# Attention followed by an MoE-style layer: q and k in one transfer over 128 partitions plus a small rest, and a scheduler that assumes later landings

## The chip, the core and the metric

The kernel runs on one core of a Trainium2 chip. The metric is the device time of one execution in microseconds (us). All inputs and the output lie in the chip's memory (DRAM); the working memory has 128 partitions, and a transfer (DMA) writes rows of bytes into partitions.

## The reference

Everything is float32 except the two weights, which arrive as float64 and are turned into float32 on the chip.

```python
# q, k, v: (8 batches, 8 heads, 576, 64); p: (8, 8, 32, 64); scale = 1/8
p_packed = softmax(scale * p @ k.T) @ v          # 32 packed rows a head
out      = softmax(scale * q @ p_packed.T) @ p_packed
x = out.transpose(0, 2, 1, 3).reshape(8 * 576, 512)
h = x @ w_in                                     # 512 -> 2048
g = h * tanh(softplus(h))                        # mish
return g @ w_out                                 # 2048 -> 512
```

## The kernel before

Heads stand in two groups (g = 0, 1) of four. For one batch b and one group the kernel holds q and k transposed, in tiles named `xT` of 128 partitions by 4 x 320 columns. Partitions 0 to 63 hold the 64 features of the first 256 positions of the four heads, partitions 64 to 127 hold the same features of the remaining 320 positions. This is `PARTS = (0, 256), (256, 576)`; a loop over `u` walks the two parts. `load_turned` fetches such a tile with two transfers, one for each part: `k_a` (64 partitions, 4096 bytes in each, 256 KB) and `k_b` (64 partitions, 5120 bytes in each, 320 KB); `q_a` and `q_b` likewise. `load_v` fetches v as `v_main` (128 partitions of 4096 bytes, 512 KB) and `v_rest` (64 partitions of 1024 bytes, 64 KB). `load_p` fetches the packed queries (`pT`, 128 KB).

Attention of a batch: `products` (line 290) multiplies p with k into `ps_s`, or the packed values with q into `ps_s`/`ps_m`; row maxima, exponentials and sums follow on DVE and ACT; `turn_chunks` (L376, L377) turns the weights with matmuls against the identity; ACT copies them out (`a1T`, L386/L400); `values` (L413) multiplies by v; the result `pp` is turned into `ppT`. In batch 0 (method `first`, then `turned`) the products with q are copied out by ACT (L499), turned by PE (`ps_t`, L507), normalised row by row on DVE (L520 to L550) and turned by PE once more, from which ACT (L564) and DVE (L567) make `aT_hi` and `aT_lo`, a high and a low part of the attention weights. In the other batches (method `later`) DVE does the turning (L451, L574).

The layer after it is folded: `pack` (L668) multiplies `ppT` with four blocks of w_in (`wi`) into `ps_w`, from which ACT and DVE make `wp_hi` and `wp_lo`. A block of the layer is `up` (L748: `ps_h` from aT and wp, two halves of six matmuls), `gate` (L758: mish on ACT), `high` and `low` (g_hi, g_lo) and, two blocks later, `down` (L800 to L802: four chunks of three matmuls into `acc`). There are 16 blocks a batch; the 128 blocks run as batch 0 blocks 0 to 7, batch 1 blocks 0 to 15, batch 0 blocks 8 to 15, and then batches 2 to 7.

The weights come as float64 in tiles `w_st` of 128 partitions by 4096 bytes (512 KB). Each is converted by two instructions on ACT (L607, L611) and four on DVE (L614, L620, L624, L630); a w_out tile needs one more of each. There are 16 fetches of w_in and 16 of w_out. Converted w_in blocks are stored to DRAM (L633) and fetched again later (L660).

Every transfer is issued by one queue, SP. A transfer that reuses one of the eight completion counters first waits for the previous transfer on that counter, so about eight are in flight. The order of all instructions on PE, DVE, ACT and SP is made before the launch by a list scheduler, `Lineup`: `forward` walks through the operations with assumed costs and picks the next one for each engine. For a transfer it assumes that the data are there 500 ns after the time at which `wire` (a running sum of bytes over a rate) has passed; line 154 holds that number. The engines then run their queues strictly in that order; each instruction waits by semaphore for what it reads.

Of the kernel before, what the change touches and what calls it, by code (L numbers as in the profile page):

```python
# [8 lines left out]
F32 = mybir.dt.float32  # L9
# [27 lines left out]
class Lineup:  # L37
# [5 lines left out]
    AHEAD = 4000  # L43
    SWITCH = 1283
    STOP = 100
    ENGINES = ("PE", "DVE", "ACT", "SP")

    def __init__(self, slots):
# [51 lines left out]
    def forward(self, due):  # L100
        ops = self.ops
        free = {pool: [0.0] * n for pool, n in self.slots.items()}
        at = {e: 0.0 for e in self.ENGINES}
        wire, warm, table = 0.0, 0.0, "exp"
        begins, ends, tooks = {}, {}, {}
        left, left_users = [len(op["needs"] | op["behind"]) for op in ops], {k: set(v) for k, v in self.users.items()}
        pool_of, last = {}, {}
        est = {n: 0.0 for n, op in enumerate(ops) if not left[n]}
        while est:
            best = {}  # L110
            for n, begin in est.items():
                op = ops[n]
                begin = max(begin, at[op["engine"]])
                wanted = {}
                for pool, _ in op["takes"]:
                    wanted[pool] = wanted.get(pool, 0) + 1
                if any(len(free[pool]) < k for pool, k in wanted.items()):
                    continue
                for pool, k in wanted.items():
                    begin = max(begin, sorted(free[pool])[k - 1] + self.HOP)  # L120
                if op["engine"] == "SP":
                    begin = max(begin, wire - self.AHEAD, op["never_before"])
                cost = begin
                if op["table"] and op["table"] != table and due[n] > begin:
                    cost += self.SWITCH
                best.setdefault(op["engine"], []).append((cost, due[n], n, begin))
            if not best:
                raise RuntimeError("stuck: " + ", ".join(str(ops[n]["takes"]) for n in sorted(est)))
            picks = []
            for engine, found in best.items():  # L130
                first = min(found)[0]
                d, n, cost, begin = min((d, n, c, b) for c, d, n, b in found if c <= first + self.NEAR)
                picks.append((cost, d, n, begin))
            cost, _, n, begin = min(picks)
            op = ops[n]
            del est[n]
            took = op["cost"]
            tooks[n] = took
            if op["table"] and op["table"] != table:
                table = op["table"]  # L140
                begin += self.SWITCH
                tooks[n] += self.SWITCH
            if op["engine"] == "PE":
                if begin > at["PE"]:
                    took += self.STOP
                if begin - at["PE"] > 2500:
                    warm = begin + 4000
                if begin < warm:
                    took = min(2 * took, (took + (warm - begin) / 2) if begin + 2 * took > warm else 2 * took)
            begins[n] = begin  # L150
            at[op["engine"]] = begin + took
            if op["engine"] == "SP":
                wire = max(wire, begin + 1500) + op["lag"]
                ends[n] = wire + 500
            else:
                ends[n] = begin + took + op["lag"]
            for pool, k in op["takes"]:
                free[pool].remove(min(free[pool]))
                pool_of[k] = pool
            for k in op["uses"]:  # L160
                left_users[k].discard(n)
                last[k] = max(last.get(k, 0.0), ends[n])
                if not left_users[k]:
                    free[pool_of[k]].append(last[k])
            for m in op["after"]:
                left[m] -= 1
                if not left[m]:
                    est[m] = max((ends[w] + self.HOP for w in ops[m]["needs"]), default=0.0)
        assert len(begins) == len(ops), len(begins)
        return begins, ends, tooks  # L170
# [9 lines left out]
def body(  # L180
    ctx: ExitStack,
    tc: tile.TileContext,
    q_a: bass.AP,
    q_b: bass.AP,
    k_a: bass.AP,
    k_b: bass.AP,
    v_main: bass.AP,
    v_rest: bass.AP,
    pT: bass.AP,
# [5 lines left out]

    nc = tc.nc

    B, G, D, H4, CUT = q_a.shape  # L200
    NP = 32
    S = CUT + q_b.shape[4]
    HALF = S // 2
    PARTS = (0, CUT), (CUT, S)
    DF = w_in.shape[1]
    DO = w_out.shape[1]
    P = 128
    NF = DF // P
    FC = 512
    NCH = S // P  # L210
    MAIN = NCH * P
    REST = S - MAIN
    scale = 1.0 / float(D) ** 0.5
# [8 lines left out]
    ps_h = ctx.enter_context(tc.tile_pool(name="ps_h", bufs=1, space=bass.MemoryType.PSUM))  # L222
# [5 lines left out]
    make_identity(nc, ident)  # L228


    ps_warm = ps_h.tile([P, P], F32, name="ps_warm", tag="ps_x")

    wo = {i: const.tile([P, 2, DO], F32R, name=f"wo{i}") for i in range(NF // 2)}

# [15 lines left out]
    class Batch:  # L250
# [10 lines left out]

        def load_turned(self, ts, src, g):
            ts[g] = att.tile([P, H4 * (S - CUT)], F32, name="xT", tag="T", bufs=XB)
            for u, (a, e) in enumerate(PARTS):
                nc.sync.dma_start(
                    out=ts[g][u * D:(u + 1) * D, :H4 * (e - a)].rearrange("a (h t) -> a h t", h=H4), in_=src[u][self.b, g]
                )

        def load_k(self, g):
            self.load_turned(self.kT, (k_a, k_b), g)  # L270

        def load_q(self, g):
            self.load_turned(self.qT, (q_a, q_b), g)

        def load_v(self, g):
            t = self.v[g] = att.tile([P, NCH + 1, H4, D], F32, name="v", bufs=VB)
# [3 lines left out]
        def begin(self):  # L280
            self.a1 = att.tile([P, 2, S], F32, name="a1", tag="a", bufs=2)
            self.pp = att.tile([P, 2, 2, D], F32, name="pp")
            self.rs = stat.tile([P, 2], F32, name="rs")
            self.sums = stat.tile([P, 2, 2], F32, name="sums")
# [880 lines left out]
def by_slot(x):  # L1165

    import numpy as np

    x = np.asarray(x)
    b, h, s, d = x.shape  # L1170
    x = x.reshape(b, 2, h // 4, 2, s, d)
    return np.stack([x[:, 0], x[:, 1][:, :, ::-1]], axis=1).reshape(b, 2, 4, s, d)


def laid_out(q, k, v, p, moe_w_in, moe_w_out):

    import numpy as np

    def turned(x, a, e):
        return by_slot(x)[..., a:e, :].transpose(0, 1, 4, 2, 3)  # L1180

    s = q.shape[2]
    cut = s // 128 * 64
    vs = by_slot(v)
    b, g, h, _, d = vs.shape
    main = s // 128 * 128
    ps = by_slot(p).transpose(0, 4, 1, 2, 3).reshape(b, d, g, -1)
    return {
        "q_a": turned(q, 0, cut),
        "q_b": turned(q, cut, s),  # L1190
        "k_a": turned(k, 0, cut),
        "k_b": turned(k, cut, s),
        "v_main": vs[:, :, :, :main].reshape(b, g, h, main // 128, 128, d).transpose(0, 1, 4, 3, 2, 5),
        "v_rest": vs[:, :, :, main:].transpose(0, 1, 3, 2, 4),
        "pT": np.concatenate([ps, ps], axis=1),
        "w_in": moe_w_in,
        "w_out": moe_w_out,
    }
# [22 lines left out]
```

## Time and profile before

| | |
|---|---|
| median of 3 runs | 734.15 us (732.8 to 736.47) |
| the profiled execution | 735.77 us, span of the program in it 734.0 us |
| busy: PE, DVE, ACT | 712.8, 393.1, 301.3 us |
| granted TensorE clock, mean | 0.976 |
| bytes moved | 85.74 MB, mean 117 GB/s |
| q and k transfers | 64 in all (16 each of q_a, q_b, k_a, k_b) |

PE is TensorE, DVE VectorE, ACT ScalarE; "PEld" is the loading of weights into TensorE. The span is the time from the program's first to its last instruction; the profiled execution's own time is 1.8 us longer. A profile lists work by line of the kernel and by the names of the tiles (out<-in). "Idle before <-X" means that the engine stood still and that X ended the wait. A busy PE counts overlapping matmuls, so its busy time says that it had work, not that it ran at its peak.

### The profile page before, as it was taken

To read this page: it belongs to the slowest core of one execution; us is meant where nothing else is said; L and a number is where in the kernel's file an instruction comes from. 1 tells how busy PE (TensorE), PEld (TensorE's weight loads), DVE (VectorE), ACT (ScalarE), POOL (GpSimd) and SP (SyncE) were. 2 spreads that over 40 slices of the span, in tenths; PEclk is the share of its full clock that TensorE was granted. 3 is DMA by queue.
4 is the path that set the end of the run, shared out by engine and by line. 5 is a ranking of instruction groups with operands and counts; after the bars stand their busy time and mean duration, and the time that the engine had idled before them with its cause. 6 is when DMAs were issued, how large, how long until landed. Compare 5 with 4: busy or idle time off the path is not lost.

```text
span 734.0 us, 12404 instructions
## 1 busy us (share of the span) xinstructions
PE 712.8 (97%) x5058; PEld 572.0 (78%) x5058; DVE 393.1 (54%) x702; ACT 301.3 (41%) x718; POOL 0.7 (0%) x6
## 2 busy tenths in 40 slices
PE   6679999999999999999999999999999999999997
PEld 4267787878787878887788787877788787888886
DVE  4589988955743446353743537343564445542332
ACT  4488776543521434243422425225333254332221
POOL 0000000000000000000000000000000000000000
PEclk7579999999999999999999999999999999999999
DMA  9994066732318310671115611292013911130002
GB/s 266 276 320 171 6 225 203 223 98 80 115 44 226 119 50 9 190 183 59 58 58 150 183 57 58 60 274 97 7 52 116 270 61 58 58 115 1 1 1 72
DMA packets 27833, 85.74 MB, mean 117 GB/s; under 512 B 3712, under 2 KB 5760, under 8 KB 27776
## 3 DMA queue, kind: packets, MB, share of 16 engines
q1 hardware_dynamic: 27776, 84.95, 38.4%
q8 instruction: 40, 0.66, 0.4%
q14 instruction: 17, 0.14, 0.1%
HBM read 71.30 MB, written 13.63 MB: 116 GB/s over the span
## 4 chain that ended last, share of the span: by engine, by line
PE 88%; DMA 8%; ACT 2%; DVE 1%; issue 0%; SPq 0%; ACTq 0%
PE ps_h L748 27%; PE acc L800 16%; PE acc L801 15%; PE acc L802 15%; PE ps_w L668 4%; DMA w_st<-in_w_in_dram 4%; PE ps_rest L800 2%; PE ps_rest L801 2%; PE ps_rest L802 2%; PE ps_pp L413 2%; DMA xT<-in_k_b_dram 2%; DMA xT<-in_q_b_dram 1%; DMA w_st<-in_w_out_dram 1%; PE ps_m L290 1%; PE ps_s L290 1%; PE ps_a L376 1%
## 5 line engine op out<-in xcount | busy, mean ns | idle before, releaser
L758 ACT ACTIVATE g<-ps_h 128x288 f32<-128x288 f32 (+1 forms) x256 | 98.5, 386 | 295.5 <-PE ps_h L748 212.2
L800 PE MATMUL acc<-wo,g_hi 128*128 128x512 f32 x512 | 203.9, 398 | 0.0
L801 PE MATMUL acc<-wo,g_hi 128*128 128x512 f32 x512 | 201.7, 394 | 0.0
L802 PE MATMUL acc<-wo,g_lo 128*128 128x512 f32 x512 | 201.1, 393 | 0.0
L748 PE MATMUL ps_h<-aT_hi,wp_hi 128*128 128x288 f32 x512 | 155.7, 304 | 0.3 <-DVE a L451 0.3
L748 PE MATMUL ps_h<-aT_hi,wp_lo 128*128 128x288 f32 x512 | 151.7, 296 | 0.2 <-DVE wp_lo L685 0.2
L748 PE MATMUL ps_h<-aT_lo,wp_hi 128*128 128x288 f32 x512 | 151.4, 296 | 0.0
L766 DVE CAST g_hi<-g 128x512 fp32r<-128x512 f32 x112 | 47.3, 422 | 180.5 <-ACT g L758 180.2
L748 PEld LDWEIGHTS ps_h<-aT_hi,wp_hi 128*128 128x128 f32 x512 | 96.6, 189 | 34.9 <-issue 24.2
L802 PEld LDWEIGHTS acc<-wo,g_lo 128*128 128x128 f32 x512 | 96.0, 188 | 23.0 <-DVE g_lo L770 0.2
L800 PEld LDWEIGHTS acc<-wo,g_hi 128*128 128x128 f32 x512 | 96.0, 188 | 19.6 <-DVE g_hi L766 3.4
L801 PEld LDWEIGHTS acc<-wo,g_hi 128*128 128x128 f32 x512 | 96.1, 188 | 11.0
L748 PEld LDWEIGHTS ps_h<-aT_lo,wp_hi 128*128 128x128 f32 x512 | 96.7, 189 | 9.0
L748 PEld LDWEIGHTS ps_h<-aT_hi,wp_lo 128*128 128x128 f32 x512 | 96.7, 189 | 0.6 <-DVE wp_lo L685 0.6
L770 DVE TENSOR_TENSOR g_lo<-g,g_hi 128x512 fp32r<-128x512 f32 x128 | 88.3, 690 | 6.4 <-ACT g_hi L766 0.4
L685 DVE TENSOR_TENSOR wp_lo<-ps_w,wp_hi 128x512 fp32r<-128x512 f32 x64 | 41.6, 684 | 40.7 <-ACT wp_hi L680 40.6
L680 ACT CAST wp_hi<-ps_w 128x512 fp32r<-128x512 f32 x64 | 34.5, 590 | 40.6 <-PE ps_w L668 40.6
L668 PE MATMUL ps_w<-wi,ppT 64*32 64x512 f32 x512 | 36.7, 615 | 0.0
L760 ACT ACTIVATE g_rest<-ps_h 128x64 f32<-128x64 f32 x128 | 28.0, 219 | 0.0
L800 PE MATMUL ps_rest<-wo,r_hi 128*128 128x512 f32 x64 | 25.1, 392 | 0.0
L801 PE MATMUL ps_rest<-wo,r_hi 128*128 128x512 f32 x64 | 25.1, 392 | 0.0
L802 PE MATMUL ps_rest<-wo,r_lo 128*128 128x512 f32 x64 | 25.1, 392 | 0.0
(97 smaller groups left out, 566.9 us busy)
## 6 DMA issues: line engine op xcount, KB each, us to landing
wi<-w_in_f SPq DMA_DIRECT2D x48, 512.0 KB, 4.8
w_st<-in_w_in_dram SPq DMA_DIRECT2D x16, 512.0 KB, 8.2
v<-in_v_main_dram SPq DMA_DIRECT2D x16, 512.0 KB, 8.4
w_st<-in_w_out_dram SPq DMA_DIRECT2D x16, 512.0 KB, 6.8
out_dram<-o SPq DMA_DIRECT2D x32, 256.0 KB, 2.2
xT<-in_k_b_dram SPq DMA_DIRECT2D x16, 320.0 KB, 6.4
xT<-in_q_b_dram SPq DMA_DIRECT2D x16, 320.0 KB, 8.9
xT<-in_k_a_dram SPq DMA_DIRECT2D x16, 256.0 KB, 5.5
```

Source lines behind the costliest of these rows:

```text
L290: nc.tensor.matmul(out=out[u][h * NP:(h + 1) * NP], lhsT=packT[u * D:(u + 1) * D, h * NP:(h + 1) * NP], rhs=xT[u * D:(u + 1) * D, h * (e - ...
L668: nc.tensor.matmul(out=ps[h * NP:(h + 1) * NP, g, :], lhsT=ppTb[row:row + D, g, h * NP:(h + 1) * NP], rhs=wis[c, g][row:row + D, h // 2, : ...
L680: nc.scalar.copy(out=hi, in_=fresh[b, c][:, g])
L685: nc.vector.tensor_tensor(out=lo, in0=fresh[b, c][:, g], in1=hi.bitcast(F32), op=ALU.subtract)
L748: nc.tensor.matmul(out=ps, lhsT=w[:, fs], rhs=a[:, g, cs], start=(n == 0), stop=(n == 5))
L758: nc.scalar.activation(out=self.act[:, hf * HALF:hf * HALF + m], in_=ps[:, :m], func=AF.Mish)
L760: nc.scalar.activation(out=self.g_rest[self.b % 2, self.f // 4][:, self.f % 4, :], in_=ps[:, m:], func=AF.Mish)
L766: cast(out=self.g[0], in_=self.act)
L770: nc.vector.tensor_tensor(out=lo, in0=self.act, in1=hi.bitcast(F32), op=ALU.subtract)
L800: nc.tensor.matmul(out=acc, lhsT=hi[:, cs], rhs=wh, start=start, stop=False)
L801: nc.tensor.matmul(out=acc, lhsT=hi[:, cs], rhs=wl, start=False, stop=False)
L802: nc.tensor.matmul(out=acc, lhsT=lo[:, cs], rhs=wh, start=False, stop=stop)
```

## The change

The host lays q and k out so that one row of DRAM for each of 128 partitions holds 1024 float32: for partitions 0 to 63 the first part, for partitions 64 to 127 the first 1024 of the second part's 1280 columns. These go in one transfer (`q_main`, `k_main`: 128 partitions of 4096 bytes, 512 KB). The last 256 columns of the second part go in another (`q_rest`, `k_rest`: 64 partitions of 1024 bytes, 64 KB). The tile in the working memory is the same as before, byte for byte, and so is all the arithmetic. In the scheduler the assumed landing moves from 500 to 2000 ns after `wire`. The tile of the eight warm-up matmuls moves to another slot of the same pool.

```diff
 class Lineup:
+    LATE = 2000
...
             if op["engine"] == "SP":
                 wire = max(wire, begin + 1500) + op["lag"]
-                ends[n] = wire + 500
+                ends[n] = wire + self.LATE
...
-    ps_warm = ps_h.tile([P, P], F32, name="ps_warm", tag="ps_x")
+    ps_warm = ps_h.tile([P, P], F32, name="ps_warm", tag="ps_h")
...
         def load_turned(self, ts, src, g):
             ts[g] = att.tile([P, H4 * (S - CUT)], F32, name="xT", tag="T", bufs=XB)
-            for u, (a, e) in enumerate(PARTS):
-                nc.sync.dma_start(
-                    out=ts[g][u * D:(u + 1) * D, :H4 * (e - a)].rearrange("a (h t) -> a h t", h=H4), in_=src[u][self.b, g]
-                )
+            nc.sync.dma_start(out=ts[g][:, :H4 * CUT], in_=src[0][self.b, g])
+            nc.sync.dma_start(out=ts[g][D:, H4 * CUT:], in_=src[1][self.b, g])
...
-    def turned(x, a, e):
-        return by_slot(x)[..., a:e, :].transpose(0, 1, 4, 2, 3)
+    def turned(x):
+        x = by_slot(x).transpose(0, 1, 4, 2, 3)
+        b, g, d, h, _ = x.shape
+        first, second = (y.reshape(b, g, d, -1) for y in (x[..., :cut], x[..., cut:]))
+        n = h * cut
+        return np.concatenate([first, second[..., :n]], axis=2), second[..., n:]
```

Three places show how the instructions move. The lines of the changed kernel are numbered a few higher (L601 is L603 there), and buffer numbers in names differ.

First, SP's queue near its beginning, where q of batch 0 (and the first w_out tile) is fetched. Before:

```order
L601 DMA w_st<-in_w_in_dram 128x1024
L265 DMA xT<-in_q_a_dram 64x1024
L265 DMA xT<-in_q_b_dram 64x1280
L601 DMA w_st<-in_w_out_dram 128x1024
L260 DMA pT<-in_pT_dram 128x256
```

And after:

```order
L603 DMA w_st<-in_w_in_dram 128x1024
L268 DMA xT<-in_q_main_dram 128x1024
L269 DMA xT<-in_q_rest_dram 64x256
L603 DMA w_st<-in_w_out_dram 128x1024
L264 DMA pT<-in_pT_dram 128x256
```

The second q pair, between w_out and pT, reads like the first and is left out in both. The places in the queue are the same; each pair of half-width transfers has become a full-width one and a small one. SP's first 35 rows keep their order; behind them some stores and fetches of weights change places.

Second, PE's queue at the first products with k (batch 0, group 0 and then group 1), with the waits. Before:

```order
L290 MATMUL ps_s<-xT,pT 32x256 [waits DMAHW2_49,DMAHW1_49]
L290 MATMUL ps_s<-xT,pT 32x256 x3
L290 MATMUL ps_s<-xT,pT 32x320 [waits DMAHW3_49]
L290 MATMUL ps_s<-xT,pT 32x320 x3
L290 MATMUL ps_s<-xT,pT 32x256 [waits DMAHW4_49]
```

And after:

```order
L292 MATMUL ps_s<-xT,pT 32x256 [waits DMAHW2_49,DMAHW1_49]
L292 MATMUL ps_s<-xT,pT 32x256 x3
L292 MATMUL ps_s<-xT,pT 32x320 x3
L292 MATMUL ps_s<-xT,pT 32x320 [waits DMAHW3_49]
L292 MATMUL ps_s<-xT,pT 32x256 [waits DMAHW4_49]
```

The order of PE's matmuls is the same in both kernels, over the whole program. What moved is the wait for the second transfer: from the first of the second part's four matmuls to the last.

Third, ACT's queue in the conversion of the last w_in tiles (L607 and L611 before, L609 and L613 after), between the two half gates of block 14, counted from 0 (`g<-ps_h`). Before:

```order
L607 ACTIVATE wi<-w_st 128x512
L611 ACTIVATE wround<-w_st 128x512
L718 COPY o_rest<-ps_rest 128x512
L607 ACTIVATE wi<-w_st 128x512
L758 ACTIVATE g<-ps_h_1331 128x224
L760 ACTIVATE g_rest_1204<-ps_h_1331 128x64
L611 ACTIVATE wround<-w_st 128x512
L766 CAST g_hi<-g 128x512
```

And after:

```order
L609 ACTIVATE wi<-w_st 128x512
L613 ACTIVATE wround<-w_st 128x512
L720 COPY o_rest<-ps_rest 128x512
L760 ACTIVATE g<-ps_h_1316 128x224
L762 ACTIVATE g_rest_1192<-ps_h_1316 128x64
L768 CAST g_hi<-g 128x512
L609 ACTIVATE wi<-w_st 128x512
L613 ACTIVATE wround<-w_st 128x512
```

The conversion now stands behind the gate and the cast to g_hi, where it stood ahead of them. Moves of this kind fill rows 123 to 204 of ACT's queue and rows 139 to 224 of DVE's; ahead of these rows and behind them both queues keep their order.

More of the change, by code (lines that the diff above doesn't have):

```diff
@@ L182, in body @@
     tc: tile.TileContext,
[L183 to L186, printed above, removed]
+    q_main: bass.AP,
+    q_rest: bass.AP,
+    k_main: bass.AP,
+    k_rest: bass.AP,
     v_main: bass.AP,
@@ L198, in body @@
     nc = tc.nc
-    B, G, D, H4, CUT = q_a.shape
+    B, G, D, LEFT = q_rest.shape
+    H4 = 4
     NP = 32
-    S = CUT + q_b.shape[4]
+    CUT = q_main.shape[3] // H4
+    S = 2 * CUT + LEFT // H4
     HALF = S // 2
@@ L263, in load_turned @@
             ts[g] = att.tile([P, H4 * (S - CUT)], F32, name="xT", tag="T", bufs=XB)
-            for u, (a, e) in enumerate(PARTS):
-                nc.sync.dma_start(
-                    out=ts[g][u * D:(u + 1) * D, :H4 * (e - a)].rearrange("a (h t) -> a h t", h=H4), in_=src[u][self.b, g]
-                )
+            nc.sync.dma_start(out=ts[g][:, :H4 * CUT], in_=src[0][self.b, g])
+            nc.sync.dma_start(out=ts[g][D:, H4 * CUT:], in_=src[1][self.b, g])
         def load_k(self, g):
-            self.load_turned(self.kT, (k_a, k_b), g)
+            self.load_turned(self.kT, (k_main, k_rest), g)
         def load_q(self, g):
-            self.load_turned(self.qT, (q_a, q_b), g)
+            self.load_turned(self.qT, (q_main, q_rest), g)
         def load_v(self, g):
@@ L1177, in laid_out @@
     import numpy as np
-    def turned(x, a, e):
-        return by_slot(x)[..., a:e, :].transpose(0, 1, 4, 2, 3)
     s = q.shape[2]
     cut = s // 128 * 64
+    def turned(x):
[4 more added lines that the diff above has]
+        return np.concatenate([first, second[..., :n]], axis=2), second[..., n:]
+    q_main, q_rest = turned(q)
+    k_main, k_rest = turned(k)
     vs = by_slot(v)
@@ L1188, in laid_out @@
     return {
[L1189 to L1192, printed above, removed]
+        "q_main": q_main,
+        "q_rest": q_rest,
+        "k_main": k_main,
+        "k_rest": k_rest,
         "v_main": vs[:, :, :, :main].reshape(b, g, h, main // 128, 128, d).transpose(0, 1, 4, 3, 2, 5),
```

## The prediction

> **What bounds the kernel now.** I read the page's shares and slices first, then the chain of waits, then the busy times by stretch, then the three compute engines in the stretch that is left.
>
> ```profile
> PE 712.8 (97%) x5058; PEld 572.0 (78%) x5058; DVE 393.1 (54%) x702; ACT 301.3 (41%) x718; POOL 0.7 (0%) x6
> DMA  9994066732318310671115611292013911130002
> PE 88%; DMA 8%; ACT 2%; DVE 1%; issue 0%; SPq 0%; ACTq 0%
> ```
>
> PE carries 88% of the chain that ended last, and DMA 8%, which is 59 us. The slices put saturated DMA at the start. The chain in order of time shows it there (start, us, what):
>
> ```profile
> 4.18 7.85 DMA w_st<-in_w_in_dram
> 12.04 9.80 DMA xT<-in_q_b_dram
> 21.86 11.87 DMA xT<-in_k_b_dram
> 33.75 9.82 DMA w_st<-in_w_in_dram
> ...
> 44.27 0.97 ACT a1T L400 x2
> 45.28 1.94 PE ps_pp L413 x80
> 47.23 3.05 PE ps_h L748 x12
> ```
>
> Up to 43.57 us (33.75 + 9.82) each transfer in the chain is issued when one before it has landed (4.18 + 7.85 = 12.03; 12.04 + 9.80 = 21.84): the transfers alone set the pace. Then the first blocks of the big layer start, at 47.2. By stretch (window: length, busy PE, PEld, DVE, ACT, POOL, PEclk, DMA share, GB/s):
>
> ```profile
> 5.00:9.00 4.00, 1.51 (x17) 0.34 (x16) 2.65 (x6) 1.15 (x2) 0.00 (x0) 1.00 1.00 236
> 10.00:17.00 7.00, 5.24 (x54) 2.51 (x50) 4.48 (x15) 4.95 (x14) 0.00 (x0) 0.50 1.03 351
> 18.00:31.00 13.00, 9.58 (x88) 3.71 (x78) 6.04 (x11) 5.97 (x15) 0.00 (x0) 0.50 1.03 239
> 31.00:38.00 7.00, 3.07 (x36) 1.15 (x34) 6.34 (x16) 3.57 (x6) 0.00 (x0) 0.74 1.03 350
> 38.00:44.00 6.00, 4.21 (x19) 3.85 (x19) 4.95 (x16) 4.18 (x12) 0.00 (x0) 0.57 1.04 300
> 44.00:50.00 6.00, 4.71 (x92) 4.20 (x93) 5.85 (x14) 4.57 (x10) 0.00 (x0) 0.72 1.03 265
> 50.00:60.00 10.00, 9.71 (x91) 6.90 (x90) 9.39 (x19) 8.70 (x22) 0.00 (x0) 1.00 1.02 410
> 90.00:150.00 60.00, 59.80 (x337) 49.75 (x336) 51.33 (x97) 38.50 (x90) 0.00 (x0) 1.00 0.70 214
> 150.00:720.00 570.00, 570.00 (x4069) 463.25 (x4068) 267.05 (x455) 199.95 (x490) 0.00 (x0) 1.00 0.31 92
> ```
>
> Three things are to be seen. From 50 us on PE is never without work for more than a few tenths, and in 150 to 720 not at all, with DMA at 31%: a faster transfer buys nothing there. Before that PE has work for less than half of some stretches (1.51 of 4.0 us, 3.07 of 7.0), much of it at half clock. And in those 50 us DMA is always busy, yet moves 350 GB/s in some stretches and 236 to 239 in others. The slow stretches are those of the 64-partition transfers: 5 to 9 us holds k of batch 0, and 18 to 31 both q pairs of batch 0 and both k pairs of batch 1, a w_out tile and pT, which by their sizes are 4 x 0.590 + 0.524 + 0.131 = 3.01 MB, against 13.0 x 239 = 3.11 MB moved. The stretches at 350 hold w_st and v, whose rows are as long (4096 bytes) but go to 128 partitions, the small v_rest included.
>
> **The change, part by part.** *The transfers.* Each of 32 loads was 256 KB and 320 KB and becomes 512 KB and 64 KB: as many transfers, as many bytes, as many issues. Its shape is then that of a v load (v_main and v_rest). No row shows q or k in it; the bounds are no gain (239 GB/s stays) and the rate of full-width tiles with no small transfers among them, 410 GB/s (50 to 60 us). I take 350, the rate of the two stretches that hold v loads. At 350 the slow stretches shrink: 5 to 9 by 4.0 x (1 - 236/350) = 1.30 us, 18 to 31 by 13.0 x (1 - 239/350) = 4.12, and 38 to 43.57 (q of batch 1) by 5.57 x (1 - 300/350) = 0.80. The transfer that lands at 43.57 would land 6.2 us earlier. At 410 it would be 1.70 + 1.01 + 5.42 + 1.02 + 1.49 = 10.6, the five stretches from 5 to 43.57 in turn.
>
> [...]
>
> *What the compute makes of it.* Earlier data help only as far as the engines in order waited for them. From PE, ACT and DVE (start, us, engine, work, and in brackets the idle time before it and what ended it):
>
> ```profile
> 22.86 2.12 PE L668 MATMUL ps_w<-wi,ppT 64*32 64x512 f32 x12
> 26.89 1.08 PE L290 MATMUL ps_s<-xT,ppT 64*32 64x256 f32 x8 [1.91 <-DMA xT<-in_q_a_dram]
> 28.37 1.29 PE L290 MATMUL ps_s<-xT,ppT 64*32 64x320 f32 x8 [0.40 <-DMA xT<-in_q_b_dram]
> ...
> 39.12 1.09 PE L507 MATMUL ps_t<-ident,a 128*128 128x128 f32 x4 [4.61 <-DVE a L550]
> ```
>
> ```profile
> 18.90 0.66 ACT L607 ACTIVATE wi<-w_st 128x512 f32<-128x512 f32 x1 [0.93 <-DMA w_st<-in_w_in_dram]
> ...
> 34.89 0.66 ACT L607 ACTIVATE wo<-w_st 128x512 f32<-128x512 f32 x1 [1.52 <-DMA w_st<-in_w_out_dram]
> ...
> 41.13 0.67 ACT L607 ACTIVATE wi<-w_st 128x512 f32<-128x512 f32 x1 [0.95 <-DMA w_st<-in_w_in_dram]
> ...
> 43.59 0.68 ACT L607 ACTIVATE wi<-w_st 128x512 f32<-128x512 f32 x1 [0.73 <-DMA w_st<-in_w_in_dram]
> 44.16 1.07 ACT L400 COPY a1T<-ps_a 128x512 f32<-128x512 f32 x2
> ```
>
> ```profile
> 30.74 0.69 DVE L520 TENSOR_REDUCE small<-ps_t 128x16 f32<-128x512 f32 x1 [1.03 <-PE ps_t L507]
> ...
> 36.76 0.82 DVE L541 TENSOR_REDUCE small<-a 128x20 f32<-128x640 f32 x1 [0.62 <-ACT a L537]
> ```
>
> 1. ACT waits at 18.90 for the fourth w_in tile ahead of the last copies of batch 0's attention. It lands 1.30 us earlier, so everything up to PE's pack moves by 1.30; the pack ends at 24.98 - 1.30 = 23.7.
> 2. The second q pair, used from 26.89 and 28.37 on, lands 1.30 + (28.37 - 18) x 0.317 = 4.6 us earlier, at 23.8. PE starts it at 23.8 (3.1 earlier), and the 0.40 inside goes too, since the rest is wanted by the last matmul only: 3.5.
> 3. DVE works without a break from 30.74 to the second turn on PE (39.12), but for 0.62 at 36.76, where ACT held the exponentials behind the wait at 34.89. That tile lands over 5 us earlier: 3.5 + 0.6 = 4.1.
> 4. ACT waits at 41.13 and 43.59 (0.95 + 0.73) ahead of the two a1T copies at 44.16 on which PE's next step hangs. Both tiles land about 6 us earlier, and the waits go: 4.1 + 1.7 = 5.8. The last tile allows 6.2, so it doesn't stop this.
>
> PE enters the dense stretch **5.8 us earlier**. Late next are DVE's aT_lo and g_lo, which have moved by 4.1 + 0.95 or so; the first g_lo was idle before it for 0.40 us, so a few tenths can be lost there. I leave 5.8.
>
> *The assumed landing and the warm-up tile.* PE's order is unchanged, and so are the first 123 rows of ACT and 139 of DVE, that is, everything up to about 90 us. Behind that conversions stand later, often behind a gate and not ahead of it. What it can win is what PE lost there, and what it can lose is bounded by the waits of ACT for landings in 60 to 150 us (us in total, times, longest):
>
> ```profile
> ACT wi L607 <- DMA w_st<-in_w_in_dram: 5.9, 5, 2.2
> ACT wo L607 <- DMA w_st<-in_w_out_dram: 5.7, 5, 1.6
> ...
> PE ps_h L748 <- DVE wp_lo L685: 0.2, 1, 0.2
> ```
>
> ACT waited 11.6 us, and PE lost 0.2: the gates have slack of more than such a wait. I take 0, with +0.2 and -11.6 as ends. One late fetch of w_out now stands behind k and half of v of batch 2 on SP, 1.9 MB or about 5.4 us at 350 GB/s; it is the last of the sixteen tiles and wanted last, so I cost it nothing. The warm-up tile's other slot costs nothing, since PE runs the warm-up matmuls ahead of all else.
>
> *Sum.* 735.77 - 5.8 = 730.0 for an execution like the profiled one, which was 1.6 above the median. On the median, 734.15 - 5.8 = **728.3 us**. One unknown has both signs: the clock. In 44 to 50 us it was granted at 0.72, full from 50. At half clock for 0.56 x 6 = 3.4 us PE does half the work, so 1.7 us were lost there; a start at another moment can lose up to as much again, or none of it.
>
> **The rivals.** *A, more.* If q and k run at 410 GB/s: step 1 gives 2.7 (1.70 + 1.01), step 2 PE's pack ends at 22.3 and the data are there (4.6 + 0.4 = 5.0), step 3 0.6 and step 4 1.7: 7.3, 726.9 us. For it: the pure full-width stretch. Against it: small transfers stay in the mix.
>
> *B, the engines keep it.* At half clock (PEclk 0.50 to 31 us) and with DVE unbroken after 30.74, only steps 1 and 2's wait of 1.91 pay, and ACT's later waits turn into waits for PE and DVE: 3.2 us, 731.0 us. For it: DVE busy 6.34 of 7.0 us in 31 to 38. Against it: the brackets on ACT name transfers.
>
> *C, no change.* If not the width but the layout of q and k in DRAM makes them slow, 239 GB/s stays: 734.2. Against it: w_st and v rows have the same length in DRAM. [...]
>
> *D, slower.* The moved conversions put landings ahead of gates that PE needs, in 90 to 150 us. If all 11.6 us of ACT's waits reached PE, 734.15 - 5.8 + 11.6 = 740.0 us. It is slower than before once more than half of them arrive at PE. Against it: 0.2 us arrived before, and the changed order puts gates first.
>
> *E, slower by the rests.* If each small transfer stopped the stream for its fixed part, the nearest row is a transfer issued alone:
>
> ```profile
> 90.20 3.98 DMA w_st<-in_w_in_dram
> ```
>
> Less 0.524 MB at 410 GB/s (1.28 us) it leaves 2.7 us, for six rests 16.2: 734.15 - 6.2 + 16.2 = 744.2 us; from 1.0 us a rest on nothing is won. Against it: two v loads, each with such a rest, land within 10 to 17 us, and the stretch runs at 351 GB/s. [...]
>
> **How the numbers follow.** Forecast 0.52, A 0.21, B 0.14, C 0.07, D 0.04, E 0.02. The forecast's and A's cases are faster by over 0.5% (3.7 us, about what a measurement of this kernel can tell from no change), with a small part of the forecast's spread falling short and a part of B's reaching it: faster 0.74, within 0.5% 0.20, slower 0.06. The range goes from A with the clock's 1.7 and a little of its own spread (724.5) to B with a fraction of the clock's loss (731.8); C, D and E, 0.13, lie outside, and some tails.
>
> **What would show it.** In the changed kernel the stretches of q and k run at about 350 GB/s, with no band at 236 to 239; PE's first ps_h starts near 41.4 and not at 47.2; the bracket of 1.91 before the second q products is gone, and so are ACT's at 41.13 and 43.59; from there to the end the trace lasts as long as before (687 us). Wrong would be: GB/s still near 240 (C), ACT or DVE waiting for PE in 25 to 45 us (B), PE with idle time for wp_lo, g_lo or a gate in 85 to 145 (D).

## The result, and the profile after

| | before | after |
|---|---|---|
| median of 5 runs, us | 734.69 (732.8 to 736.69) | 728.39 (727.55 to 729.86) |
| ratio to before, 95% interval | 1 | 0.9913 [0.989, 0.9936] |
| the profiled execution, us | 735.77, span 734.0 | 729.13, span 727.4 |
| granted TensorE clock, mean | 0.976 | 0.99 |
| first `ps_h` of the dense stretch, us | 47.16 | 40.43 |
| from there to the end of the span, us | 686.84 | 686.97 |

The changed kernel takes 6.3 us less, and the last two rows say where: in the two profiled executions all of it lies ahead of the first block of the big layer. Among the experiments below, one of three_wide's five executions took 1537.69 us, and its ratio goes by the other four. From the page of the profile after, the busy times, the DMA slices and the shares of the chain that ended last:

```profile
PE 709.9 (98%) x5058; PEld 572.0 (79%) x5058; DVE 393.3 (54%) x702; ACT 302.4 (42%) x718; POOL 0.7 (0%) x6
DMA  9990255812228111721118203271105611130002
PE 89%; DMA 5%; DVE 3%; ACT 1%; issue 0%; SPq 0%; DVEq 0%; ACTq 0%
```

DMA's share of the chain fell from 8% to 5%, and DVE's rose from 1% to 3%. The slices (18 us each) show that DMA is saturated in the first three in both kernels (9, 9, 9), and that what was left in the fourth, 4 tenths, is gone. The chain in order of time (start, us, what):

```profile
3.90 7.01 DMA w_st<-in_w_in_dram
...
15.04 2.81 PE ps_pp L415 x80
...
18.76 7.39 DMA xT<-in_k_main_dram
26.17 7.67 DMA w_st<-in_w_in_dram
...
34.44 0.58 ACT aT_hi L566
35.05 0.69 DVE aT_lo L569
...
37.03 0.59 ACT a1T L402
37.67 2.83 PE ps_pp L415 x80
40.50 3.19 PE ps_h L750 x12
```

Before, transfers alone set the pace up to 43.57 us. Now they do so in two pieces, and compute sits between them and behind them. The same stretches as before (length, busy PE, PEld, DVE, ACT, POOL, granted clock, DMA share, GB/s):

```profile
5.00:9.00 4.00, 1.30 (x17) 0.30 (x16) 2.27 (x5) 0.90 (x2) 0.00 (x0) 1.00 0.98 321
10.00:17.00 7.00, 5.85 (x91) 3.17 (x79) 5.64 (x17) 5.62 (x15) 0.00 (x0) 1.00 1.03 374
18.00:31.00 13.00, 8.43 (x91) 3.27 (x90) 11.41 (x25) 9.08 (x20) 0.00 (x0) 0.98 1.04 357
31.00:38.00 7.00, 4.62 (x33) 4.17 (x37) 6.21 (x20) 5.76 (x16) 0.00 (x0) 0.50 1.03 362
38.00:44.00 6.00, 6.00 (x92) 5.30 (x84) 5.68 (x12) 3.45 (x9) 0.00 (x0) 0.50 1.03 377
```

The band at 236 to 239 GB/s is gone: 5 to 9 us runs at 321 and 18 to 31 at 357. In the latter DVE is busy for 11.41 of 13.0 us where it was busy for 6.04. PE is now at work throughout 38 to 44 us, but at half clock. PE, ACT and DVE at the places that the prediction's steps name (start, us, engine, work, and the idle time before it with what ended it):

```profile
20.09 2.17 PE L670 MATMUL ps_w<-wi,ppT 64*32 64x512 f32 x16
22.31 1.52 PE L292 MATMUL ps_s<-xT,ppT 64*32 64x256 f32 x16
23.76 1.20 PE L509 MATMUL ps_t<-ident,a 128*128 128x128 f32 x9
...
32.12 1.09 PE L509 MATMUL ps_t<-ident,a 128*128 128x128 f32 x4 [4.82 <-DVE a L552]
...
37.67 2.83 PE L415 MATMUL ps_pp<-v,a1T 128*32 128x64 f32 x80 [1.27 <-ACT a1T L402]
40.43 0.61 PE L750 MATMUL ps_h<-aT_hi,wp_hi 128*128 128x288 f32 x1
```

```profile
17.00 0.69 ACT L609 ACTIVATE wi<-w_st 128x512 f32<-128x512 f32 x1
...
20.16 0.67 ACT L609 ACTIVATE wo<-w_st 128x512 f32<-128x512 f32 x1 [0.98 <-DMA w_st<-in_w_out_dram]
...
33.87 0.68 ACT L609 ACTIVATE wi<-w_st 128x512 f32<-128x512 f32 x1 [0.70 <-DMA w_st<-in_w_in_dram]
...
35.49 0.67 ACT L609 ACTIVATE wi<-w_st 128x512 f32<-128x512 f32 x1
36.06 0.57 ACT L402 COPY a1T<-ps_a 128x512 f32<-128x512 f32 x1
37.03 0.59 ACT L402 COPY a1T<-ps_a 128x512 f32<-128x512 f32 x1 [0.41 <-DVE a1T L405]
```

```profile
29.77 0.81 DVE L543 TENSOR_REDUCE small<-a 128x20 f32<-128x640 f32 x1
...
31.34 1.36 DVE L552 TENSOR_TENSOR a<-a,small 128x512 f32<-128x512 f32 x2
```

PE starts the second q products right behind its pack, without the 1.91 us of waiting that stood there, and DVE's gap of 0.62 us is gone too. Of ACT's two waits for w_in tiles one is left (0.70 us at 33.87), and a new one has come, for DVE (0.41 us at 37.03).

The wait at 20.16 stands at a place that the prediction's steps leave out. Before, it was ACT's longest in this stretch:

```profile
25.97 0.66 ACT L607 ACTIVATE wo<-w_st 128x512 f32<-128x512 f32 x1 [5.22 <-DMA w_st<-in_w_out_dram]
```

This is the first w_out tile. Its conversion stands in ACT's queue ahead of the copies of the q products (L499 before, L501 after). It landed at 25.89 us before and at 20.08 after, and the copies start at 26.53 and 20.74.

### The profile page after: what moved, and what is told of

It is laid out like the page before. It is cut to its first block, busy times and chain, and to the rows that moved or that the text cites. A ratio compares the mean times of both kernels' runs of the same rounds, so it can differ in the third digit from the quotient of the medians.

```text
span 727.4 us, 12407 instructions
## 1 busy us (share of the span) xinstructions
PE 709.9 (98%) x5058; PEld 572.0 (79%) x5058; DVE 393.3 (54%) x702; ACT 302.4 (42%) x718; POOL 0.7 (0%) x6
## 4 chain that ended last, share of the span: by engine, by line
PE 89%; DMA 5%; DVE 3%; ACT 1%; issue 0%; SPq 0%; DVEq 0%; ACTq 0%
PE ps_h L750 28%; PE acc L802 16%; PE acc L803 15%; PE acc L804 15%; PE ps_w L670 4%; PE ps_pp L415 2%; DMA w_st<-in_w_in_dram 2%; PE ps_rest L802 2%; PE ps_rest L803 2%; PE ps_rest L804 2%; DMA w_st<-in_w_out_dram 1%; PE ps_m L292 1%; DMA xT<-in_k_main_dram 1%; PE ps_a L378 1%; PE ps_s L292 1%
```

## The experiments

Times are medians, ratios are to the kernel before on the same chip. The kernels were run in three groups, each on one chip: the first four, the next three, the last four. The kernel before had medians of 735.19, 735.25 and 735.01 us there.

| kernel | us | ratio [95%] | first `ps_h`, us | 18 to 31 us, GB/s |
|---|---|---|---|---|
| late_only | 735.43 | 1.0002 [0.9993, 1.0011] | 44.97 | 243 |
| transfers_only | 729.13 | 0.9919 [0.9907, 0.9931] | 39.29 | 359 |
| three_narrow | 735.56 | 1.0004 [0.9994, 1.0015] | 44.46 | 252 |
| three_wide | 729.9 | 0.9928 [0.9914, 0.9941] | 42.01 | 329 |
| rest_twice | 731.67 | 0.9954 [0.9935, 0.9972] | 41.91 | 332 |
| one_full | 726.27 | 0.9888 [0.9866, 0.991] | 39.52 | 379 |
| filler | 729.31 | 0.9913 [0.9895, 0.9932] | 39.36 | 358 |
| one_full, assumed landing 500 | 727.86 | 0.9901 [0.9887, 0.9914] | 38.13 | 388 |
| one_full again | 727.16 | 0.989 [0.9877, 0.9904] | 38.17 | 384 |
| the changed kernel again | 728.1 | 0.9906 [0.9893, 0.9918] | 40.10 | 354 |
| transfers_only again | 728.89 | 0.9919 [0.9905, 0.9932] | 41.55 | 343 |

The first ps_h and the GB/s are those of one profiled execution each, and they differ between executions of the same transfers: the first ps_h by 2.2 us between the kernel before (47.16) and late_only (44.97), and by 2.3 us among the four profiles of the changed kernel and transfers_only (39.29 to 41.55).

### The two halves of the change

late_only is the kernel before with the scheduler's new assumption alone:

```diff
-                ends[n] = wire + 500
+                ends[n] = wire + 2000
```

> The transfers of before, with the assumed landing of 2000 ns alone. My theory (the landing assumption costs and brings nothing): the time of before, about 734.7 us, within 1.5 us either way, and PE's first ps_h near 47.2 us. Rival (the new order of conversions on ACT and DVE brings the gain or a good part of it): 728 to 732 us, with the gain behind 90 us, since the order ahead of that is unchanged.

transfers_only is the changed kernel with the old assumption:

```diff
-    LATE = 2000
+    LATE = 500
```

> The changed transfers with the old assumed landing of 500 ns, so the engines' order is that of before. My theory: the whole gain, 728.4 us within 1.0 us, first ps_h near 40.4 us. Rival (the two parts of the change need each other): 730 to 734 us, with new idle time on PE between 85 and 145 us.

The transfers are the whole gain: 0.9919 [0.9907, 0.9931] with them alone, 1.0002 [0.9993, 1.0011] without them. The times were as expected; the first ps_h was 2.2 us earlier than expected in late_only and 1.1 in transfers_only. From late_only's chain:

```profile
30.89 8.59 DMA w_st<-in_w_in_dram
...
45.04 3.19 PE ps_h L748 x12
```

This tile lands at 39.48 us, against 41.11 before, and the next w_in tile at 41.13, against 43.57, out of the same transfers in the same order. So the profile of before is a late one in this stretch.

That the assumption costs nothing net is not the same as that it does nothing. In late_only the last w_out tile is fetched behind k and half of v of batch 2, and the trace shows a chain from its landing to PE, in this order on ACT, DVE and PE:

```profile
146.74 0.66 ACT L607 ACTIVATE wo<-w_st 128x512 f32<-128x512 f32 x1 [2.07 <-DMA w_st<-in_w_out_dram]
```

```profile
147.44 0.43 DVE L614 TENSOR_SCALAR wo<-wo 128x512 f32<-128x512 f32 x1 [2.85 <-ACT wo L607]
...
153.18 1.42 DVE L363 TENSOR_TENSOR a<-ps_s,top 128x512 f32<-128x512 f32 x2
```

```profile
154.02 0.37 PE L748 MATMUL ps_h<-aT_hi,wp_hi 128*128 128x288 f32 x1 [1.28 <-DVE a L363]
```

ACT stands for 2.07 us for the tile, DVE for 2.85 for ACT, and DVE's queue then holds the tile's whole conversion ahead of batch 2's subtraction (L363), for which PE waits 1.28 us. From the start of ACT's conversion to PE's start it is 154.02 - 146.74 = 7.28 us. The same chain is in the changed kernel, where the tile lands earlier against PE's own progress:

```profile
140.57 0.66 ACT L609 ACTIVATE wo<-w_st 128x512 f32<-128x512 f32 x1 [0.38 <-DMA w_st<-in_w_out_dram]
```

```profile
147.84 0.37 PE L750 MATMUL ps_h<-aT_hi,wp_hi 128*128 128x288 f32 x1 [0.31 <-DVE a L365]
```

That is 7.27 us, with 0.31 left for PE to wait. The other side is the assumption's gain: with 500 the profiles show PE waiting for wp_lo at an earlier place, 0.2 us in the kernel before and 0.4 and 0.3 in the two of transfers_only, and with 2000 they do not. What the assumption does is also seen in ACT's waits between 60 and 150 us (us in total, times, longest). In late_only 2.7 us are left of the 11.6 before (2.5 for w_out, 0.2 for w_in), and ACT waits for PE instead (14.8 us, where it was 5.2):

```profile
ACT g L758 <- PE ps_h L748: 14.8, 19, 2.1
...
ACT wo L607 <- DMA w_st<-in_w_out_dram: 2.5, 2, 2.1
```

Nine microseconds less of ACT's waiting for transfers, and no time gained: they were slack, as the prediction took them to be.

### Width, or the number and length of rows

three_narrow cuts the main transfer in two by partitions, so that q and k come in three transfers of 64 partitions. Tile, bytes and DRAM layout are those of the changed kernel:

```diff
-            nc.sync.dma_start(out=ts[g][:, :H4 * CUT], in_=src[0][self.b, g])
+            for u in range(2):
+                nc.sync.dma_start(out=ts[g][u * D:(u + 1) * D, :H4 * CUT], in_=src[0][self.b, g, u * D:(u + 1) * D])
```

> As the changed kernel, but the full-width transfer of each k and q is issued as its two halves, 64 partitions of 4096 bytes each; the layout in DRAM and the small rest stay. Theory (the number of partitions sets the rate): back to about 240 GB/s in 5 to 9 and 18 to 31 us, and 734 to 736 us. Rival (layout in DRAM, or the split into 512 and 64 KB): 728 to 730 us and about 350 GB/s.

three_wide cuts it by columns, into two transfers of 128 partitions by 2048 bytes:

```diff
-            nc.sync.dma_start(out=ts[g][:, :H4 * CUT], in_=src[0][self.b, g])
+            for u in range(2):
+                c = slice(u * 2 * CUT, (u + 1) * 2 * CUT)
+                nc.sync.dma_start(out=ts[g][:, c], in_=src[0][self.b, g, :, c])
```

> As the run before it, with as many transfers of the same sizes, but the main part is cut by columns: two transfers of 128 partitions with 2048 bytes in each. Theory (partitions set the rate): 728 to 729.5 us and 340 to 360 GB/s in 18 to 31 us. Rival (rows of 4096 bytes, or transfers of 512 KB, are what is fast): 731 to 735 us and below 300 GB/s.

The stretches 5 to 9 and 18 to 31 us of three_narrow, and then those of three_wide, in the columns used above:

```profile
5.00:9.00 4.00, 2.30 (x17) 0.60 (x16) 2.58 (x5) 1.17 (x2) 0.00 (x0) 1.00 1.06 236
18.00:31.00 13.00, 10.28 (x83) 4.30 (x83) 9.15 (x17) 6.50 (x16) 0.00 (x0) 0.71 1.05 252
```

```profile
5.00:9.00 4.00, 2.23 (x21) 0.65 (x20) 3.16 (x7) 0.96 (x2) 0.00 (x0) 0.92 1.00 333
18.00:31.00 13.00, 8.40 (x91) 3.43 (x91) 11.01 (x20) 8.41 (x19) 0.00 (x0) 0.76 1.00 329
```

The two move the same bytes in the same number of transfers, out of the same DRAM layout, and into the same tile. With 64 partitions the rate is 236 to 252 GB/s and the time that of the kernel before; with 128 it is 329 to 333 and nearly all of the gain is there. So it is the width, not the layout in DRAM and not the number of transfers. three_wide missed its expectation narrowly, by 0.4 us and by 11 GB/s in 18 to 31 us; whether its shorter rows or its one transfer more a load cost that is not shown. three_narrow's 236 and 252 GB/s are those of stretches that mix halves with full-width tiles.

### What the small rest costs

rest_twice fetches each rest a second time, into the lower 64 partitions, where nothing reads it:

```diff
             nc.sync.dma_start(out=ts[g][D:, H4 * CUT:], in_=src[1][self.b, g])
+            nc.sync.dma_start(out=ts[g][:D, H4 * CUT:], in_=src[1][self.b, g])
```

> As the changed kernel, but each small rest of q and k is sent a second time, into the lower 64 partitions of the same columns, which nothing reads: one more transfer of 64 KB a load, six of them ahead of the transfers that gate the first ps_h. My theory (the fixed part of a small transfer is hidden, it costs its bytes): 0.2 to 0.35 us each, first ps_h 0.5 to 2 us later, 728.9 to 730.5 us. [...]

one_full moves the same bytes as rest_twice in one transfer of 128 partitions by 5120 bytes for each tile (640 KB), the lower half's last 1024 bytes being such unread columns:

```diff
-            nc.sync.dma_start(out=ts[g][:, :H4 * CUT], in_=src[0][self.b, g])
-            nc.sync.dma_start(out=ts[g][D:, H4 * CUT:], in_=src[1][self.b, g])
+            nc.sync.dma_start(out=ts[g], in_=src[self.b, g])
```

> The same bytes as the run with each rest sent twice, in one transfer: 128 partitions of 5120 bytes (640 KB), of which the lower half's last 1024 bytes are read by nothing. The count of transfers is a third. Theory (bytes and partitions count, not transfers): within 1 us of the run with the rest sent twice, 728.5 to 730 us. Rival (a transfer has its price in line): 726 us or less, below the changed kernel too.

Both expectations missed. rest_twice was slower than its upper end of 730.5 by 1.2 us, and the two kernels that were to be within 1 us of each other are 5.4 apart. The w_in tile that landed at 43.57 us before, and at 35.12 in the changed kernel, lands at 37.48 in rest_twice and at 35.31 in one_full. Six second rests ahead of it cost 37.48 - 35.12 = 2.36 us, 0.39 each, of which their 64 KB at the changed kernel's 357 GB/s are 0.18. So a small transfer costs some 0.2 us beyond its bytes here, with about eight in flight (in the changed kernel the transfer issued at 3.90 us lands at 10.91, and the eighth behind it is issued at 10.92). In the other profiles with the changed transfers the tile lands at 34.54 to 36.28, by which it is 0.0 to 0.3 us. Against one_full, which moves the same bytes in twelve fewer transfers up to there and lands the tile at 35.31 in this profile and at 33.77 in the second one below, it is 0.2 to 0.3. The prediction's price was nothing beyond the bytes, and its rival E's 2.7 us: it is near the former and no longer negligible over many. In one_full's first profile the 64 KB more a tile cost as much as the small transfer that they replace: the stretch runs at 379 GB/s and the tile lands within 0.2 us of the changed kernel's; in the second it lands 1.35 us earlier.

The landings in the first two profiles differ by 2.2 us (37.48 - 35.31), and the first ps_h by 2.4. That is less than half of the 5.4 us between the medians; what the rest is made of is open. The two profiles can't say, since they are of executions of 730.29 and 729.56 us, which are only 0.7 apart.

### The half clock

In the first profile of the changed kernel TensorE's granted clock is a half from 30.4 to 44.1 us, ahead of the dense stretch and into it. filler lets PE run 20 matmuls of the identity into the unused warm-up tile behind batch 1's products with k, where PE waited 4.82 us for DVE:

```diff
             self.s_all = self.all_products(self.pT, self.kT, "ps_s")
+            if self.b == 1:
+                for _ in range(20):
+                    nc.tensor.matmul(out=ps_warm, lhsT=ident, rhs=ident, start=True, stop=True)
```

> The changed kernel with 20 matmuls of the identity by itself added on PE, into a spare tile, behind the products of batch 1 with k, where PE stood idle for about 5 us before the second turn of batch 0; their results are not used. Theory (the idle time took the granted clock down to a half between 30 and 44 us, and 1.8 us of PE's dense work and 0.9 of ps_pp were lost to it): clock full through 30 to 44 us, 726 to 727.5 us. Rival (ACT, DVE and the transfers set that stretch, the clock is no matter): 728 to 729 us, with PE faster but idle longer.

The stretches of filler, cut at the moment when its clock falls:

```profile
17.50:38.00 20.50, 15.10 (x193) 10.01 (x192) 18.10 (x43) 14.86 (x36) 0.00 (x0) 1.00 1.04 366
38.00:41.40 3.40, 3.40 (x52) 3.06 (x49) 3.40 (x8) 1.88 (x4) 0.00 (x0) 0.50 1.04 394
```

In this profile the clock is what it was to be: full up to 38.0 us, where the four profiles of the changed kernel and transfers_only have a mean of 0.76 to 0.98 from 18 to 31 us. That the matmuls did it is not shown by one profile; rest_twice, without them, has 1.00 from 18 to 31 us too, and 0.51 from 31 to 38. And filler brought nothing that the medians show, 0.9913 [0.9895, 0.9932] against the changed kernel's 0.9913 and 0.9906; the intervals leave room for about 1 us. In the changed kernel DVE is busy for 11.41 of the 13 us from 18 to 31, and PE waits for it; the rival of this run, that ACT, DVE and the transfers set this stretch, fits. The theory that the half clock costs 1 to 2 us of the median has no support: the 726 to 727.5 us that it gave did not come.

### One chip for four versions

one_full with the old assumption, and one_full, the changed kernel and transfers_only once more, unchanged, to compare the four on one chip. The one new edit, in one_full:

```diff
-    LATE = 2000
+    LATE = 500
```

> One transfer of 640 KB a load, with the old assumed landing of 500 ns. Theory (with 2000 ns the last w_out tile is fetched behind k and half of v of batch 2, ACT and DVE wait for it, and PE stands up to 1.3 us near 150 us): no wait of PE for the subtraction of batch 2's maxima, 0.3 to 1.5 us below the same transfers with 2000 ns. Rival (that wait is covered in most executions): the same time as with 2000 ns.

> The kernel with one transfer of 640 KB a load once more, beside the changed kernel on the same chip. Theory (a small transfer has a price of about 0.2 us in line beyond its bytes): 1 to 3 us below the changed kernel, ratio to before 0.987 to 0.991. Rival (the 2 us between them in separate runs were the clock's moments): within 0.7 us of the changed kernel.

> The changed kernel itself beside the others, on the same chip: 728 to 729.5 us, with PE's first ps_h between 39.3 and 42 us, depending on the moments at which the clock is granted, and a wait of PE for batch 2's subtraction of 0.2 to 1.3 us.

> The changed transfers with 500 ns again, beside the changed kernel on the same chip. Theory (2000 ns wins about 0.5 us near 120 us and loses 0.3 to 1.5 near 150): 0 to 1 us below the changed kernel. Rival: equal within 0.3 us, or above it.

The old assumption was to be better, by 0.3 to 1.5 us in one_full and by 0 to 1 us with two transfers, since the 1.3 us wait near 150 us was in the first one_full. It was not: 727.86 with 500 against 727.16 with 2000 in one_full, and 728.89 against 728.1 with two transfers. Both are 0.7 to 0.8 us the other way, with intervals that overlap. In one_full with 500 the profile shows what it costs: PE waits 0.7 us each for wp_hi and wp_lo, and with 2000 for neither. The wait near 150 us depends on the execution: the same kernel one_full had it in its first profile, where the last w_out tile took 9.14 us from issue to landing, and not in its second, where it took 7.16. PE's row in the first:

```profile
148.25 0.37 PE L748 MATMUL ps_h<-aT_hi,wp_hi 128*128 128x288 f32 x1 [1.30 <-DVE a L363]
```

one_full has the lowest median in both groups in which it ran, 727.16 against 728.1 us for the changed kernel where both did. The intervals of the two overlap, so its lead of about 1 us (1 to 3 were expected) is likely and not shown; it beats the kernel before by 1.1% in both groups. Why it isn't more is in its chain. From the second profile of one_full (start, us, what):

```profile
2.58 7.64 DMA w_st<-in_w_in_dram
10.24 9.82 DMA w_st<-in_w_out_dram
20.15 0.68 ACT wo L607
...
30.78 1.27 DVE a L550 x2
...
36.33 1.95 PE ps_pp L413 x80
```

The last transfer in it is the first w_out tile, which lands at 20.06 us. From there to the dense stretch DVE and ACT carry the chain. So it is in the second profile of the changed kernel too, and in filler's:

```profile
12.23 9.04 DMA w_st<-in_w_out_dram
...
38.14 2.07 PE ps_pp L415 x80
```

This is the prediction's rival B, engines that keep the gain: it begins where the changed kernel stands, in some executions. The first work that reads a w_out tile (`acc`) starts at 43.0 us in the second profile of one_full, but the tile's conversion stands in the queues of ACT and DVE ahead of batch 0's normalisation. That a later place for it would win time was not tried.

## Why the prediction was right, point by point

The forecast was 728.3 us in a range of 724.5 to 731.8, and 728.39 was measured. What was forecast of the cause is shown: width sets the rate (252 GB/s from 18 to 31 us in three_narrow, 329 in three_wide), the waits for the slow tiles go, and the dense stretch starts earlier by several us and lasts as long as before. That the number agrees to 0.1 us is luck, since the start moves by 2 us between executions. The points below compare the two profiles above, 47.16 and 40.43 us; against late_only's start, 44.97, the gain is 4.5 us and not 6.7. In this pair two of the forecast's terms were off and took much of each other back.

- **The rate** was right, and in this pair the stretch to which it applied too short. 350 GB/s was forecast; from the landing of the first w_in tile to that of the one at 35.12, 10.35 MB (eight w_st, two pT, and the main and rest of four k, four v and two q) come in 30.46 us, which is 340 GB/s, where they took 38.66 us before, 268 GB/s. But the prediction cut three stretches only (5 to 9, 18 to 31, 38 to 43.57), and narrow transfers were also in flight between these: the last k pair, which landed at 33.73 before, lands its main part at 26.15 (18.76 + 7.39). So the tile came 8.45 us earlier, not 6.2. The same bytes over 350 GB/s would have given 9.1. Against late_only, where the tile lands at 41.13, it came 6.0 us earlier, and the same sum gives 6.5. So the forecast's 6.2 lies within what single executions differ by, and neither way of adding up is shown to be the better one.
- **Step 1**, the end of the pack: 22.26 (20.09 + 2.17) for 24.98, so 2.7 us and not 1.3. ACT's wait of 0.93 is gone, and PE's q products ahead of the pack start 1.6 earlier (19.23 for 20.81); the further 1.1 goes with PE's clock, 0.98 instead of 0.50 from 18 to 31 us. That is argued from the rows, not tried.
- **Step 2**, the second q products: 4.6 us earlier (22.31 for 26.89). Their data landed at 22.17 and 22.61, where 23.8 was forecast. With their inner wait gone and PE at full clock ps_t is 5.8 earlier (23.76 for 29.59), against 3.5. It needs ACT's copies of the products too, and that these came 5.8 us earlier hangs on the first w_out tile, which the step does not name.
- **Step 3**, DVE's gap of 0.62: gone, as forecast, so that the scaled weights are 7.0 us earlier (31.34 for 38.35). The step's own term was right; what it added to was larger.
- **Step 4**, ACT's two waits: half right. One is gone, of the other 0.70 of 0.95 us is still there, since the engines came earlier by about as much as the tile did (33.87 for 41.13). The a1T copies start 8.1 us earlier, but the second waits 0.41 for DVE, and PE's ps_pp is 7.6 earlier.
- **The clock** took part of it back. ps_pp took 2.83 us at half clock where it took 1.94, so the first ps_h is 6.73 us earlier and not 7.6; 5.8 was forecast. The clock was named as an unknown with both signs of up to 1.7 us, and 0.9 of it came. Before, the half clock lay in three pieces, with short full ones between them (the granted clock is the third number from the end):

```profile
9.00:32.90 23.90, 18.52 (x185) 8.14 (x189) 14.12 (x33) 11.74 (x31) 0.00 (x0) 0.50 1.03 282
36.30:43.10 6.80, 3.98 (x19) 3.85 (x19) 5.25 (x17) 5.30 (x14) 0.00 (x0) 0.50 1.04 321
46.50:50.00 3.50, 3.50 (x40) 3.16 (x29) 3.50 (x8) 2.68 (x5) 0.00 (x0) 0.51 1.03 284
```

- **The assumed landing**, costed at 0: right in sum, 1.0002 [0.9993, 1.0011]. The late fetch of w_out, which was to cost nothing because it is wanted last, is wanted earlier than that by DVE's order; it costs PE 0.31 us in the profile of the changed kernel and up to 1.30 in others, and 0.2 to 1.4 us of waits for wp_lo and wp_hi are seen with 500 alone.
- **The rivals.** C (layout, not width) is out by three_narrow and three_wide. Of D something came, at one place near 150 us and at about a tenth of its price: the conversion stood ahead of batch 2's subtraction, not of a gate. E is out by rest_twice, 0.2 us a rest beyond its bytes where 1.0 would have eaten the gain. Its own price was too high from the start: the tile at 90.20 was not issued alone, a second one followed at 90.80, and when the first landed, at 94.18, 0.88 MB had moved and not 0.52. A's rate of 410 GB/s was not reached by the stretch from 18 to 31 us of any version (357 in the changed kernel, 388 at most). A's end of the pack, 22.3 us, is that of the profile (22.26), in part for another reason, the clock. B's 731.0 us did not come, and its half clock up to 31 us is not in the first profile after; but its mechanism is near, as the chains without a transfer after 21.3 us show, and as does ACT's wait of 0.41 for DVE.

The gain held to the end: 686.84 and 686.97 us from the first ps_h on, against the forecast's 687.

## What to carry to other kernels

Where the slices show saturated DMA and the GB/s differ between stretches, look at how many partitions the transfers of the slow stretches write; joining two halves into one full-width transfer brought the tile that mattered 6 to 8 us earlier out of 36 to 39 here, and a small transfer beside it cost 0.0 to 0.3 us beyond its bytes. Work out such a gain up to the landing that matters, and then walk through all the waits that hang on it, the longest first, since the engines can take over from the transfers, as here from 20 to 21 us on in three profiles. Compare more than one profile before a microsecond is explained. A wait on an engine with slack is worth nothing, 9 us of them here; a conversion that a scheduler puts into an engine's queue ahead of critical work can be worth more than its own wait, so look at what stands behind it.

## What the runs showed of the hardware that was not expected

- With transfers of 64 partitions in the mix, 18 to 31 us ran at 239 to 252 GB/s, with those of 128 partitions at 329 to 388: rows of 2048 bytes at 329, of 4096 with one small rest a load at 343 to 359, and of 5120, without the small rests, at 379 to 388.
- A transfer of 64 KB with about eight in flight cost 0.39 us in rest_twice, 0.2 more than its bytes at 357 GB/s; by other profiles it is 0.0 to 0.3 more.
- The granted clock differs between executions, and the start of the dense stretch too. In the four profiles with two transfers a tile (transfers_only and the changed kernel, each twice) the first ps_h was at 39.29, 41.55, 40.43 and 40.10 us, with a mean clock from 18 to 31 us of 0.87, 0.76, 0.98 and 0.79 and a rate there of 359, 343, 357 and 354 GB/s. A single profile says where time goes, but its start of the dense stretch is good to some 2 us only; whether the clock sets the difference was not shown.
- With 20 more matmuls on TensorE the clock was full to 38.0 us in filler's one profile, and to 30.4 in the changed kernel's first, without an effect that the median shows.
